# A recurrent state kernel with soft experts: the triangular solver on GpSimd, the first-half Gram by batch, a-tiles by ScalarE and a new order

## The chip, the cores and the metric

The kernel runs on one core of a Trainium2 chip. Its engines are TensorE (PE in the profile; PEld is its weight load), VectorE (DVE), ScalarE (ACT), GpSimd (POOL) and SyncE (SP), which issues nearly all loads. The metric is the device time of one execution in microseconds (us).

## The reference, cut to what matters

```python
# r, k, v, w, a, b: (4, 8, 768, 40), fp32;  B, H, S, D = 4, 8, 768, 40
for t in range(S):
    y[:, :, t] = einsum('bhd,bhde->bhe', r_t, state)
    Sa = einsum('bhde,bhe->bhd', state, a_t)
    state = state * w_t[:, :, None, :] - einsum('bhd,bhe->bhde', Sa, b_t) \
            + einsum('bhd,bhe->bhde', v_t, k_t)
x = y.transpose(0, 2, 1, 3).reshape(3072, 320)
logits = x @ phi                                   # 8 experts x 4 slots
d = softmax(logits over the rows); slot_input = d.T @ x
slot_out[e] = relu(slot_input[e] @ w1[e]) @ w2[e]  # 320 -> 1024 -> 320
out = softmax(logits over the slots) @ slot_out
```

## The kernel before, in words

The 768 steps are cut into 12 stages of 64 (NST; index st), and each stage into two halves of 32 (index q). The 32 pairs of batch and head are worked on in three groups u of 3, 3 and 2 heads (NHU) with all four batches, so that a group's 120 or 80 channels stand on the partitions. Two stages make a super-stage ss of 128 steps, for which one solve is made.

Per stage the pieces are these.

- prep_items (scan_s, scan_k, scan_c): the running products of the decays by two TENSOR_TENSOR_SCANs on DVE, and three multiplications of 120x768 that scale k, b and a, on POOL but for the first stages.
- bda_at, bdr_at: block-diagonal copies of the a- and r-tiles (one head's 40 channels in its own block). For a, bd_mult makes them by three ACT multiplications with a mask in stages under BM, and bd_load by DMAs from SBUF in the others. For r it is always bd_load.
- lgram and gram: products of k and b with a. lgram gives the triangular systems (32x32, one for each batch, head and half). gram gives the rest: rows 0 to 95 for the second half of the stage, rows 96 to 127 for the first. A mask multiplication on DVE takes them from PSUM to the tile qls.
- solve_in, solve_step, solve_out: the inverse of the triangular systems of a super-stage. solve_in transposes them on DVE (STREAM_TRANSPOSE), ACT copies, 30 steps follow that each have a multiplication and an addition of i x (31 - i) elements, and solve_out transposes back. The columns 0 to JP-1 of a step are done by POOL, the others by DVE. JP is 3 for solve 0, 7 for solve 1 and 2 for solves 2 to 5.
- chain_g, chain_u (for both halves) and chain_s: the recurrence from stage to stage. chain_g reads the old state, qls and the v-tile vus, chain_u multiplies with the solved inverse, and ACT copies its result into vus; chain_s makes the new state. chain_s adds the old state to PSUM into an SBUF temporary (wt_next) and multiplies that with the decays pms.
- y_vut, y_sd, y_p, y_y: the outputs of the stage before. slots_*: every second stage, the soft-expert statistics. After the last stage come the expert matmuls and the output.

Operations aren't issued as they are written. A class Plan records them, each with its engine, an estimated duration and what it depends on. Its schedule then simulates the engines: at each step it takes the engine that can start first, and of that engine's ready operations the one of highest prio (the length of the longest path behind it). What it finds is emitted in that order, so that each engine's queue is in order of the simulated start. The written order (run_all with the windows WIN, WIN0 and PRO) decides only which operation comes first where two share a buffer. Where the plan sees PE idle, fill puts in filler matmuls on constants (lines L462 and L466). fetch models PE's instruction loading, and pace holds loads back. Nearly all other instructions bear the line of the emitting helper, L1174 in the profile.

Of the kernel before, what the change touches and what calls it, by code (L numbers as in the profile page):

```python
# [23 lines left out]
NU = 3  # L24
# [5 lines left out]
JP = (3, 7, 2)  # L30

WIN = dict(cg=(0, 0.304, 0.4, 0.601, 0.759, 1), vl=(0.623, 0.633), ct=(0, 0.01), pr=(0.17, 0.795), ba=(0.926, 0.933),
           lw=(0.991, 1), lg=(0.121, 0.307), gr=(0, 0.404), kt=(0.696, 1), yv=(0.003, 0.4), ys=(0, 0.565), yp=(0.233,
# [3 lines left out]
            ba=(0.824, 1.778), lw=(0.869, 1.012), br=(0.133, 0.821), s0=(0.643, 1.33))  # L37
KV = 3
BM, AV = 6, 2
# [59 lines left out]


class Op:
    __slots__ = ("eng", "calls", "acc", "banks", "mode", "occ", "lat", "pred", "succ", "prio", "n", "ready", "alt", "at",
                 "done", "kind", "dma", "tag", "lanes", "boost", "turn", "rec", "after")
# [41 lines left out]
class Plan:  # L145
    def __init__(self, nc, tc, banks):
        self.nc, self.tc, self.banks = nc, tc, banks
        self.ops, self.open = [], None
        self.tensor, self.vector, self.scalar, self.gpsimd, self.sync, self.either = (
            Engine(self, n) for n in ("PE", "DVE", "ACT", "POOL", "SP", "EITHER"))  # L150
        self.live, self.masks, self.tag, self.boost = {}, {}, "", 0
# [28 lines left out]
    def record(self, eng, method, a, k):  # L180
# [11 lines left out]
        if new:  # L192
            o = Op()
            o.eng, o.calls, o.acc, o.banks, o.mode, o.kind, o.dma, o.tag, o.alt = eng, [], {}, set(), mode, method, 0, self.tag, None
            o.rec, o.after = 0, None
# [23 lines left out]
        if eng == "PE":  # L219
            o.occ = self.pe_add(o, cost, lane) + 170  # L220
            o.rec += 2 if method == "transpose" or "r" in str(a[1].dtype).split(".")[-1].replace("float", "") else 4
        else:
            self.costs(o, eng, method, a, k)
# [3 lines left out]
    def pe_cost(self, method, a):  # L227
# [13 lines left out]
        return (cls(kk), c), two * max(nn * (0.862 if two == 2 else 0.45), 8 * 4 / len(lane) if c == 32 else 45), lane  # L241
# [7 lines left out]
    def costs(self, o, eng, method, a, k):  # L249
        out = a[0]  # L250
        n = 1
        for s in out.shape[1:]:
            n *= s
        src = a[1] if len(a) > 1 and not isinstance(a[1], (int, float)) else None
# [11 lines left out]
        if eng == "DVE":  # L266
            if method == "transpose":
                dve = 2130 * n / 1024
            elif method == "tensor_tensor_scan":
                dve = 155 + 2.08 * n  # L270
            elif method == "tensor_reduce":
                dve += 0
            o.occ = dve
        elif eng == "ACT":
            if method == "activation" and not isinstance(k.get("scale", 1.0), float):
                act = 270 + 0.835 * n
            o.occ = act
        elif eng == "POOL":
            o.occ = 180 + (0.75 if method == "memset" else 1.97) * n
            if n < 300 and method == "tensor_tensor":  # L280
                o.occ += 40
        else:
            o.alt = dict(ACT=act, DVE=dve)
            o.occ = act


    def depend(self):
# [18 lines left out]
        for o in reversed(self.ops):  # L306
            d = o.occ + (2000 + o.dma / 215 if o.dma else 0)
            o.prio = d + o.boost + max((s.prio + SEM.get(o.eng + s.eng, 0) for s in o.succ), default=0)

    def schedule(self):  # L310
        self.depend()
        engs = ("PE", "DVE", "ACT", "POOL", "SP")
# [10 lines left out]
        def add(o):  # L323
            e = "ACT" if o.alt else o.eng
            o.ready = max((p.done + SEM.get(p.eng + e, 0) for p in o.pred), default=0.0)
            for e in ("ACT", "DVE") if o.alt else (o.eng,):
                cand[e].add(o)

        for o in self.ops:
            for b in o.banks:  # L330
                b.left += 1
# [3 lines left out]
        while len(order) < len(self.ops):  # L335
# [6 lines left out]
            def when(o, e):  # L342

                if o.dma:
                    return max(o.ready, self.pace(o)[0])
                if e != "PE":
                    return o.ready
                for b in o.banks:
                    if b.place is None:
# [3 lines left out]
                        r = max(o.ready, bf)  # L353
# [11 lines left out]
                return o.ready  # L365
# [14 lines left out]
            t, e = best  # L380
            ok = []
            for o in cand[e]:
                r = when(o, e)
                if r is not None and r <= t + 1e-6:
# [12 lines left out]

            if o.alt:

                e = min(("ACT", "DVE"), key=lambda x: start(o, x) + o.alt[x])  # L400
                cand["ACT"].discard(o)
                cand["DVE"].discard(o)
# [5 lines left out]
            if e == "PE":  # L408
                t, o.occ = self.fetch(o, t, free[e], dma_free)
                for b in o.banks:  # L410
                    if b.place is None:
# [3 lines left out]
                        held[b.place].append([t, None, max(m.bit_length() for x in b.ops for r in x.acc.get((b, True), ()) for m in r[2:])])  # L415
# [27 lines left out]
        import os  # L443
        if os.environ.get("PLAN"):
            print("plan", self.span, busy, len(self.ops), "stall", self.stall, "PE instructions", self.seen)
        return self.order

    def fill(self, gaps, held):

        self.extra = {}  # L450
        there = max(o.done for o in self.ops if o.dma and (self.idle[1].tensor.name, True) in o.acc)
        for a, b, p, o in gaps:

            i = next((i for i, h in enumerate(held) if all(y <= a or x >= b or c <= 384 for x, y, c in h)), None)
            n = int((b - a) * FILL[1] / (225 if a > WARM else 400))
            if i is not None and n:
                self.extra[o] = (n, p.mode if p else (128, 128), self.banks[i][:, 384:512], self.idle[a > there])

# [9 lines left out]
    def fetch(self, o, t, free, dma):  # L468

        gap = t - free  # L470
        n = int(gap * FILL[1] / 225) if gap > FILL[0] else 0
        for k, a, b in ((2 * n, free, t), (o.rec, t, t + o.occ - 165)):
# [3 lines left out]
            while left > 0:  # L476
# [5 lines left out]
                if (self.seen - FETCH[1]) % FETCH[0] == 0:  # L482
                    i = (self.seen - FETCH[1]) // FETCH[0]
                    prev = self.there[-1] if self.there else 0.0
                    self.there.append(max(x + FETCH[3] + min(FETCH[5], max(0.0, dma - x)), prev + 500) + FETCH[4])
# [35 lines left out]
    def emit(self):  # L521
# [3 lines left out]
        with self.tc.manual_schedule():  # L525
            for o in self.order:
# [3 lines left out]
                for method, a, k, line in o.calls:  # L530
# [5 lines left out]
                    if o.alt:  # L536
# [34 lines left out]
def rwkv_softmoe(ctx, tc, kb, b2, aa, ww, rr, vv, consts, phi, w1, w2, out):  # L571
# [8 lines left out]
    cs_t = cst.tile([128, 419], F32, name="cs_t")  # L580
    mask_q = cs_t[:, 0:32]
    mask_l = cs_t[:, 32:64]
# [65 lines left out]
    with ExitStack() as ac:  # L648
# [22 lines left out]
        tmp_r = [part(2, n) for n in (200, 200, 240, 240)]  # L671
# [32 lines left out]
        sms, cms = (Ring(space(4) for _ in range(2)) for _ in range(2))  # L704
        n_wt = [0]
# [60 lines left out]
        def bd_load(key, bd, src):  # L766
# [47 lines left out]
        def gram(st, u):  # L814
            if u == 0:
                qls.put(st)
            nh = NHU[u]
# [38 lines left out]
        def solve_in(ss):  # L856
            lt, n_t = lt_a, n_a
            nc.vector.transpose(lt.rearrange("p i t -> p t i"), lls[ss].rearrange("p c h t -> p t (c h)"))
            jp = JP[min(ss, 2)]
            for eng, j0, j1 in ((nc.gpsimd, 0, jp), (nc.vector, jp, 32)):  # L860
# [4 lines left out]
        def solve_step(ss, i):  # L865
            lt, n_t = lt_a, n_a
            m = 31 - i
            jp = JP[min(ss, 2)]
            for eng, j0, j1, x in ((nc.gpsimd, 0, min(i, jp), 0), (nc.vector, jp, i, 2)):
# [25 lines left out]
        def chain_g(st, u, q):  # L895
# [8 lines left out]
            k = slice(96, 128) if q == 0 else slice(0, 96)  # L904
            for j in range(nh):
                for b in range(B):
                    h = 12 * u + b * nh + j
                    nc.tensor.matmul(gp[32 * b:32 * b + 32, j * D:(j + 1) * D], qls[st][k, h, :],
                                     vu[k, h * D:(h + 1) * D], start=(sold is None), stop=(sold is None or j == nh - 1))
# [18 lines left out]
        def chain_s(st, u):  # L928
# [284 lines left out]
        if True:  # L1213
# [8 lines left out]
                    (three(gram, 3), *w["g3"]), (three(kbtok, 3), *w["k3"]))  # L1222
# [4 lines left out]
        for st in range(NST):  # L1227
# [6 lines left out]
            if st == 0:  # L1234
                o += [(one(lambda: load_w(4), lambda: load_k(4)), *w["lo"]), (prep_items(4), *w["pr"]),
# [149 lines left out]
def layouts(inputs):  # L1385
# [4 lines left out]
    def chan(n, pad):  # L1390
# [3 lines left out]
        for u in range(NU):  # L1394
# [12 lines left out]
                         for u in range(NU)], axis=3)  # L1407

    vv = vv[:, [0, 1, 0]].reshape(NST, 96, -1)
    st = np.triu(np.ones((32, 32), f4), 1)  # L1410
    one = np.ones((32, 32), f4)
    mq = np.concatenate([one, one, st, st])
# [5 lines left out]
    consts = np.concatenate([mq, -np.concatenate([st] * 4), ms, np.eye(128, dtype=f4), bm, np.tile(eye, (4, 1)), np.tile(eye, (4, 4))],  # L1418
# [3 lines left out]
               rr=chan("r", 0), vv=vv, consts=consts, phi=phi, w1=inputs["moe_w1"], w2=inputs["moe_w2"])  # L1422
# [17 lines left out]
```

## Time and profile before

| | us |
|---|---|
| median of 3 runs | 475.67 |
| lowest, highest | 465.01, 476.42 |
| the profiled execution | 468.54 |
| its span, first to last instruction | 466.5 |
| PE busy | 395.2 (85%) |
| DVE busy | 327.7 (70%) |
| ACT busy | 208.8 (45%) |
| POOL busy | 205.2 (44%) |

Busy times are sums over the span and hide its stages: up to 100 us runs the prologue (loads, solves 0 and the start of 1, the first preps), from 100 to 320 us the stages with preps and solves, then the last stages, the experts and the output. Matmuls are pipelined, so a busy PE isn't one at its peak. A row of groups has line, engine, operation, output and inputs, shapes and count, then busy us and mean ns, then the idle time before and what ended it. A row of the timeline has start and length in us, and in brackets the idle time before it.

### The profile page before, as it was taken

The page shows a single profiled execution, that of the slowest core. Times are in us where ns is not written, and L with a number is a line of the kernel's source. Part 1 is how long each engine was busy: PE and PEld are TensorE (multiplying, and loading weights), DVE is VectorE, ACT ScalarE, POOL GpSimd, SP SyncE. Part 2 cuts the span into 40 slices and gives each one's busy share as a digit, 9 for nine tenths or more (in the row PEclk, how much of TensorE's full clock was granted, in tenths as well). Part 3 has the DMA queues.
Part 4 walks back from the last instruction along what each step waited for, and adds up shares of the span by engine and source line. Part 5 has one row for each costly group of instructions (what it writes and reads, how often), then busy time and mean ns, then how long its engine had stood idle before and what let it go on. Part 6 is the DMA issues. An engine that isn't in the chain of part 4 may idle for free.

```text
span 466.5 us, 21450 instructions
## 1 busy us (share of the span) xinstructions
PE 395.2 (85%) x9399; PEld 344.9 (74%) x9399; DVE 327.7 (70%) x746; ACT 208.8 (45%) x619; POOL 205.2 (44%) x410
## 2 busy tenths in 40 slices
PE   6788787888987998989999889998968989999910
PEld 6777676777886987979888878887967767745810
DVE  7789889899899899888799958971724235332210
ACT  1521524781644737157643737564426654312210
POOL 4576976988288248761389625840000000110000
PEclk9789889998999999879999999999989999989965
DMA  8996114011442523424334244576565754870176
GB/s 201 261 224 188 36 32 128 16 55 40 127 117 81 139 79 117 111 89 130 109 112 139 90 134 133 170 231 180 140 177 142 227 163 127 240 227 1 34 156 149
DMA packets 38762, 61.27 MB, mean 131 GB/s; under 512 B 4173, under 2 KB 26557, under 8 KB 38669
## 3 DMA queue, kind: packets, MB, share of 16 engines
q1 hardware_dynamic: 38669, 59.91, 46.5%
q8 instruction: 73, 1.20, 1.1%
q14 instruction: 20, 0.16, 0.1%
HBM read 54.00 MB, written 3.93 MB: 124 GB/s over the span
## 4 chain that ended last, share of the span: by engine, by line
PE 48%; DVE 25%; DMA 9%; ACT 5%; issue 5%; POOL 2%; SPq 1%; DVEq 0%; ACTq 0%; POOLq 0%
PE ps L1174 45%; DVE wt L1174 23%; ACT wt L1174 4%; PE ps L462 3%; DMA wt<-in_vv_dram 2%; POOL wt L1174 2%; DMA wt<-in_rr_dram 2%; DMA wt<-in_w_dram 2%; DMA wt<-in_kb_dram 2%; DVE mem L1174 2%; DMA wt<-in_ww_dram 1%; ACT mem L1174 1%; PE ps L466 1%; SPq L1174 1%; DMA wt<-wt 1%
## 5 line engine op out<-in xcount | busy, mean ns | idle before, releaser
L1174 PE MATMUL ps<-wt,wt 128*32 128x40 f32 (+9 forms) x4968 | 164.0, 224 | 16.2 <-issue 5.7
L1174 PEld LDWEIGHTS ps<-wt,wt 128*32 128x32 f32 (+7 forms) x4968 | 146.4, 118 | 30.2 <-issue 12.6
L1174 POOL TENSOR_TENSOR wt<-wt 128x30 f32<-128x30 f32 (+21 forms) x360 | 140.0, 389 | 59.1 <-ACT wt L1174 33.1
L1174 DVE TENSOR_TENSOR wt<-wt 128x180 f32<-128x180 f32 (+29 forms) x324 | 123.4, 381 | 7.7 <-ACT wt L1174 2.3
L1174 DVE TENSOR_TENSOR wt<-ps,cs_t 128x384 f32<-128x384 f32 (+2 forms) x120 | 62.1, 522 | 36.8 <-PE ps L1174 28.8
L1174 ACT ACTIVATE wt<-ps 32x120 f32<-32x120 f32 (+1 forms) x288 | 72.0, 250 | 24.8 <-PE ps L1174 17.3
L1174 POOL TENSOR_TENSOR wt<-wt,wt 120x768 f32<-120x768 f32 x32 | 55.7, 1749 | 48.9 <-DMA wt<-in_kb_dram 32.4
L1174 PE MATMUL ps<-cs_t,wt 120*128 120x120 f32 (+5 forms) x496 | 69.2, 274 | 7.8 <-DMA cs_t<-in_consts_dram 2.6
L1174 ACT COPY mem<-ps 120x512 f32<-120x512 f32 (+6 forms) x99 | 45.3, 480 | 67.1 <-PE ps L1174 64.5
L1174 ACT COPY wt<-ps 128x120 f32<-128x120 f32 (+3 forms) x116 | 37.9, 357 | 80.6 <-PE ps L1174 77.7
L1174 PE MATMUL ps<-wt,mem 128*32 128x160 f32 (+4 forms) x592 | 66.9, 313 | 8.3 <-DMA wt<-in_rr_dram 6.9
L1174 PEld LDWEIGHTS ps<-wt,mem 128*32 128x32 f32 (+4 forms) x592 | 55.4, 156 | 11.0 <-DVE wt L1174 3.9
L1174 PEld LDWEIGHTS ps<-cs_t,wt 120*128 120x128 f32 (+5 forms) x496 | 53.2, 141 | 12.8 <-issue 3.5
L1174 DVE TENSOR_TENSOR_SCAN wt<-wt,wt 120x780 f32<-120x780 f32 x24 | 45.4, 1900 | 4.5 <-POOL wt L1174 2.7
L1174 POOL MEMSET mem<- 128x2048 f32 x1 | 1.8, 1804 | 96.0 <-DVE mid L1174 96.0
L462 PE MATMUL ps<-cs_t 128*128 128x128 f32 x170 | 26.3, 301 | 3.7 <-DVE wt L1174 2.0
L1174 PE MATMUL ps<-wt 32*32 32x40 f32 x1536 | 25.2, 202 | 5.0 <-issue 2.4
L462 PEld LDWEIGHTS ps<-cs_t 128*128 128x128 f32 x170 | 23.2, 210 | 5.2 <-DVE wt L1174 2.1
L1174 PEld LDWEIGHTS ps<-wt 32*32 32x32 f32 x1536 | 19.1, 107 | 10.8 <-issue 3.8
L1174 PE MATMUL ps<-mem 120*32 120x120 f32 (+1 forms) x528 | 25.5, 264 | 0.0
L1174 DVE STREAM_TRANSPOSE wt<-wt 128x1024 f32<-128x1024 f32 x12 | 25.3, 2127 | 0.3
L1174 ACT COPY wt<-wt 120x768 f32<-120x768 f32 (+6 forms) x24 | 16.9, 729 | 18.7 <-DVE wt L1174 16.6
(89 smaller groups left out, 303.5 us busy)
## 6 DMA issues: line engine op xcount, KB each, us to landing
wt<-in_w_dram SPq DMA_DIRECT2D x16, 640.0 KB
wt<-in_kb_dram SPq DMA_DIRECT2D x36, 240.0 KB
wt<-in_w_dram SPq DMA_DIRECT2D x16, 512.0 KB
wt<-in_ww_dram SPq DMA_DIRECT2D x12, 366.6 KB
mem<-in_rr_dram SPq DMA_DIRECT2D x36, 120.0 KB
wt<-in_vv_dram SPq DMA_DIRECT2D x12, 320.0 KB
wt<-in_aa_dram SPq DMA_DIRECT2D x30, 120.0 KB
wt<-in_rr_dram SPq DMA_DIRECT2D x24, 120.0 KB
```

What stands on the lines that cost most here:

```text
L462: self.nc.tensor.matmul(bank, src, src, start=True, stop=True)
L466: self.nc.tensor.matmul(bank[i:i + 32], src[r, 0:32], src[r], start=True, stop=True)
L1174: nc.vector.memset(one_f, 0.0)
```

## The change

1. Solver: JP becomes (3, 7, 32, 32, 32, 32). Solves 2 to 5 are done by POOL alone, with scratch tiles of 240 elements.
2. gram: the first-half product of batch b goes to rows 32b to 32b+31 and to columns behind the others, with a tile q0s and a mask multiplication of its own; chain_g of the first half reads q0s and a second copy of v by batch (vq, one buffer). Of v, a stage loads 64 rows in two DMAs, without the 32 rows that were repeated, and vq in a third.
3. BM = NST: the a-tiles of all stages are made by ACT.
4. bd_load (now for r alone) loads each group's heads by themselves: eight DMAs instead of three.
5. chain_s adds in place in PSUM and multiplies from there. The temporaries hold q0s and vq now.
6. gram of stage 3 is written in stage 0 instead of the prologue; the windows br of stage 0 and gr are others.
7. The plan: other constants (FETCH, FILL, ISSUE); CLASH holds a DVE operation without PSUM operands until POOL's last such one is done but for 138 ns, and the other way round (190 ns); an engine may take a more urgent operation that is ready up to 130 ns later (LOOK); PE may take a short one in front of an instruction-loading stall (NARROW); fillers only in gaps over 900 ns, less by 500 ns; and 32 random changes, by their seeds, are added to the priorities.

```diff
-JP = (3, 7, 2)
+JP = (3, 7, 32, 32, 32, 32)
...
-BM, AV = 6, 2
+BM, AV = NST, 2
...
-FETCH = (256, 96, 440, 1500, 2900, 3500)
-WARM = 9000
-FILL = (300, 0.8)
-
-ISSUE = 350
+FETCH = (256, 96, 410, 1300, 2400, 4500)
+FILL = (900, 500, 225)
+
+CLASH = dict(DVE=138, POOL=190)
+
+ISSUE = 420
...
+ROUNDS = 0
+SEEDS = (3, 21, 44, 62, 119, 136, 146, 166, 184, 236, 383, 839, 894, 1144, 1277, 1468, 1487, 1602, 1732, 2303, 3675, 4128,
+         4356, 4549, 5379, 5493, 5729, 5909, 5921, 5968, 6052, 6159)
...
+LOOK = dict(PE=1, DVE=130, ACT=1, POOL=130, SP=1)
+NARROW = (150, 24, 8000)
...
     def schedule(self):
         self.depend()
+        for o, x in zip(self.ops, sum((self.noise(n) for n in SEEDS), 0 * self.noise(0))):
+            o.prio += x
...
+    def noise(self, seed):
+        r, n = np.random.default_rng(seed), len(self.ops)
+        mode, s = r.integers(4), 10 ** r.uniform(2.7, 4.3)
+        if mode == 0:
+            return r.normal(0, s, n)
...
                 if e != "PE":
-                    return o.ready
+                    p = last.get("POOL" if e == "DVE" else "DVE") if o.clash else None
+                    return max(o.ready[e], p.done - CLASH[e]) if p and p.clash else o.ready[e]
...
+    def fillers(self, gap):
+        return int((gap - FILL[1]) / FILL[2]) if gap > FILL[0] else 0
...
-            for j in range(3):
-                g = B * sum(n > j for n in NHU)
-                load(bd[40 * j:40 * j + 40, j, 0:g], src[40 * j:40 * j + 40, 0:g], nc.sync)
+            for u in range(NU):
+                g = slice(B * u, B * u + B)
+                for j in range(NHU[u]):
+                    load(bd[40 * j:40 * j + 40, j, g], src[40 * j:40 * j + 40, g])
...
             for b in range(B):
-                nc.tensor.matmul(gr[96:128, b * w:(b + 1) * w], kbt(st)[0:n, B * u + b, 0, 0], bd[0:n, 0:nh, b, 0:32], start=True, stop=True)
+                nc.tensor.matmul(gr[32 * b:32 * b + 32, 4 * w:5 * w], kbt(st)[0:n, B * u + b, 0, 0], bd[0:n, 0:nh, b, 0:32], start=True, stop=True)
             nc.vector.tensor_tensor(
-                qls[st][:, 12 * u:12 * u + 4 * nh], gr[:, 0:4 * w].rearrange("p (h t) -> p h t", t=32),
-                mask_q.unsqueeze(1).broadcast_to([128, 4 * nh, 32]), ALU.mult)
+                qls[st][0:96, 12 * u:12 * u + 4 * nh], gr[0:96, 0:4 * w].rearrange("p (h t) -> p h t", t=32),
+                mask_q[0:96].unsqueeze(1).broadcast_to([96, 4 * nh, 32]), ALU.mult)
+            nc.vector.tensor_tensor(
+                q0s[st][:, H0[u]:H0[u] + nh], gr[:, 4 * w:5 * w].rearrange("p (h t) -> p h t", t=32),
+                mask_s.unsqueeze(1).broadcast_to([128, nh, 32]), ALU.mult)
...
-            load(vu[0:32], vv[st, 0:32])
-            load(vu[64:128], vv[st, 32:96])
+            for q in range(2):
+                load(vu[64 * q:64 * q + 32], vv[st, 32 * q:32 * q + 32])
+            load(vqs.put(st), vq[st])
...
-                wt = wt_next()
-                nc.vector.tensor_tensor(wt[0:n, 0:4 * n], sp[0:n, 0:4 * n], sold[0:n, cols(u)], ALU.add)
-                nc.vector.tensor_tensor(v4(snew[0:n, cols(u)]), v4(wt[0:n, 0:4 * n]), pmb, ALU.mult)
+                nc.vector.tensor_tensor(sp[0:n, 0:4 * n], sp[0:n, 0:4 * n], sold[0:n, cols(u)], ALU.add)
+                nc.vector.tensor_tensor(v4(snew[0:n, cols(u)]), v4(sp[0:n, 0:4 * n]), pmb, ALU.mult)
```

More of the change, by code (lines that the diff above doesn't have):

```diff
@@ L145, with __init__ @@
 class Plan:
-    def __init__(self, nc, tc, banks):
-        self.nc, self.tc, self.banks = nc, tc, banks
+    def __init__(self, nc, tc, banks, own=()):
+        self.nc, self.tc, self.banks, self.own = nc, tc, banks, {t.tensor.name for t in own}
         self.ops, self.open = [], None
-        self.tensor, self.vector, self.scalar, self.gpsimd, self.sync, self.either = (
-            Engine(self, n) for n in ("PE", "DVE", "ACT", "POOL", "SP", "EITHER"))
+        self.tensor, self.vector, self.scalar, self.gpsimd, self.sync, self.either, self.both = (
+            Engine(self, n) for n in ("PE", "DVE", "ACT", "POOL", "SP", "DVE ACT", "DVE POOL"))
         self.live, self.masks, self.tag, self.boost = {}, {}, "", 0
@@ L253, in costs @@
             n *= s
+        o.clash = ("DVE" in eng or eng == "POOL") and "ACT" not in eng and method != "transpose" and (
+            not o.banks) and not any(
+            x.tensor.name in self.own for x in aps if hasattr(x, "tensor"))
         src = a[1] if len(a) > 1 and not isinstance(a[1], (int, float)) else None
@@ L265, in costs @@
         act = 160 + 0.835 * n
[L266 to L284, printed above, removed]
+        if method == "transpose":
+            dve = 2130 * n / 1024
+        elif method == "tensor_tensor_scan":
+            dve = 155 + 2.08 * n
+        if method == "activation" and not isinstance(k.get("scale", 1.0), float):
+            act = 270 + 0.835 * n
+        pool = 180 + (0.75 if method == "memset" else 1.97) * n
+        cost = dict(ACT=act, DVE=dve, POOL=pool)
+        e = eng.split()
+        o.occ = cost[e[-1]]
+        if len(e) > 1:
+            o.alt = {x: cost[x] for x in e}
+            o.eng, o.occ = e[0], cost[e[0]]
     def depend(self):
@@ L311, in schedule, with backward, forward @@
         self.depend()
+        best, spans = None, []
+        for o, x in zip(self.ops, sum((self.noise(n) for n in SEEDS), 0 * self.noise(0))):
+            o.prio += x
+        for i in range(ROUNDS + 1):
+            self.forward()
+            spans.append(round(self.span))
+            if best is None or self.span < best[0]:
+                best = (self.span, [(o, o.at, o.done, o.occ, o.eng, o.after) for o in self.order],
+                        [(b, b.place) for b in self.tenants], self.extra, self.order)
+            if i < ROUNDS:
+                self.backward()
+        self.span, ops, places, self.extra, self.order = best
+        for o, *x in ops:
+            o.at, o.done, o.occ, o.eng, o.after = x
+        for b, b.place in places:
+            pass
+        self.spans = spans
+    def noise(self, seed):
+        import numpy as np
+        names = sorted({o.who for o in self.ops})
+        who = np.array([names.index(o.who) for o in self.ops])
+        r, n = np.random.default_rng(seed), len(self.ops)
+        mode, s = r.integers(4), 10 ** r.uniform(2.7, 4.3)
+        if mode == 0:
+            return r.normal(0, s, n)
+        v, w = np.zeros(n), r.integers(len(names))
+        if mode == 1:
+            v[who == w] = r.normal(0, s)
+        elif mode == 2:
+            i = np.where(who == w)[0]
+            a = r.integers(len(i))
+            v[i[a:a + 1 + r.integers(len(i) // 6 + 1)]] = r.normal(0, s)
+        else:
+            v = r.normal(0, s, n) * (r.random(n) < 0.05)
+        return v
+    def backward(self):
+        nxt, late = {}, {}
+        for o in sorted(self.ops, key=lambda o: (-o.done, -o.at)):
+            t = min((late[s] - SEM.get(o.eng + s.eng, 0) for s in o.succ), default=self.span)
+            if o.eng != "SP":
+                t = min(t, nxt.get(o.eng, self.span))
+            late[o] = t - (o.done - o.at)
+            nxt[o.eng] = late[o] - (LINE[o.eng] if o.eng != "SP" else 0)
+            o.prio = -late[o]
+    def forward(self):
         engs = ("PE", "DVE", "ACT", "POOL", "SP")
@@ L323, in add @@
         def add(o):
-            e = "ACT" if o.alt else o.eng
-            o.ready = max((p.done + SEM.get(p.eng + e, 0) for p in o.pred), default=0.0)
-            for e in ("ACT", "DVE") if o.alt else (o.eng,):
+            o.ready = {}
+            for e in o.alt or (o.eng,):
+                o.ready[e] = max((p.done + SEM.get(p.eng + e, 0) for p in o.pred), default=0.0)
                 cand[e].add(o)
+        self.tenants = []
         for o in self.ops:
             for b in o.banks:
-                b.left += 1
+                b.place, b.left = None, len(b.ops)
+            if o.cost:
+                o.occ, o.after = o.cost, None
+        for o in self.ops:
             if not left[o]:
@@ L390, in schedule @@
                     o = max(same, key=lambda x: (x.prio, -x.n))
-            def start(o, e):
-                p = last.get(e)
-                if p is None or e == "SP":
-                    return max(free[e], when(o, e))
-                turn = o.mode != p.mode if e == "PE" else (o.turn or p.turn)
-                return max(p.done + (TURN if turn else LINE)[e], when(o, e))
+            if e == "PE" and self.wait(o, start(o, e), free[e], dma_free) > NARROW[0]:
+                few = [x for x in ok if x.rec <= NARROW[1] and x.prio > o.prio - NARROW[2]
+                       and not self.wait(x, start(x, e), free[e], dma_free)]
+                if few:
+                    o = max(few, key=lambda x: (x.prio, -x.n))
             if o.alt:
-                e = min(("ACT", "DVE"), key=lambda x: start(o, x) + o.alt[x])
-                cand["ACT"].discard(o)
-                cand["DVE"].discard(o)
+                e = min(o.alt, key=lambda x: start(o, x) + o.alt[x])
+                for x in o.alt:
+                    cand[x].discard(o)
                 o.eng = e
@@ L414, in schedule @@
                         b.place = f[1]
-                        held[b.place].append([t, None, max(m.bit_length() for x in b.ops for r in x.acc.get((b, True), ()) for m in r[2:])])
+                        self.tenants.append(b)
+                        held[b.place].append([t, None, b.width()])
                 if t - free[e] > FILL[0]:
@@ L442, in schedule @@
         self.span, self.busy = max(o.done for o in order), busy
[L443 to L446, printed above, removed]
     def fill(self, gaps, held):
@@ L451, in fill, with wait @@
         there = max(o.done for o in self.ops if o.dma and (self.idle[1].tensor.name, True) in o.acc)
+        first = max(o.at for o in self.ops if o.kind == "memset" and o.calls[0][1][0] is self.idle[0])
         for a, b, p, o in gaps:
+            if o.at < first:
+                continue
             i = next((i for i, h in enumerate(held) if all(y <= a or x >= b or c <= 384 for x, y, c in h)), None)
-            n = int((b - a) * FILL[1] / (225 if a > WARM else 400))
+            n = self.fillers(b - a)
             if i is not None and n:
                 self.extra[o] = (n, p.mode if p else (128, 128), self.banks[i][:, 384:512], self.idle[a > there])
+    def fillers(self, gap):
+        return int((gap - FILL[1]) / FILL[2]) if gap > FILL[0] else 0
+    def wait(self, o, t, free, dma):
+        was = self.seen, list(self.there), self.stall, o.occ
+        self.fetch(o, t, free, dma)
+        lost = self.stall - was[2]
+        self.seen, self.there, self.stall, o.occ = was
+        return lost
     def filler(self, n, mode, bank, src):
@@ L468, in fetch @@
     def fetch(self, o, t, free, dma):
-        gap = t - free
-        n = int(gap * FILL[1] / 225) if gap > FILL[0] else 0
+        n = self.fillers(t - free)
         for k, a, b in ((2 * n, free, t), (o.rec, t, t + o.occ - 165)):
@@ L535, in emit @@
                     k = {n: self.place(x) for n, x in k.items()}
-                    if o.alt:
+                    if o.alt and "ACT" in o.alt:
                         s = k.get("scale")
@@ L704, in rwkv_softmoe @@
         sms, cms = (Ring(space(4) for _ in range(2)) for _ in range(2))
+        q0s = Ring(ht(t) for t in (part(3, 256), wts_t.tiles[0][:, 0:256], wts_t.tiles[0][:, 256:512]))
+        vqs = Ring([wts_t.tiles[1][:, 0:320]])
         n_wt = [0]
@@ L816, in gram @@
                 qls.put(st)
+                q0s.put(st)
             nh = NHU[u]
```

77 lines of the change are left out of this document (48 added, 29 removed).

## The prediction

> **What bounds the kernel now.** I read the page's busy shares and slices first, then the windows, the transposes that open and close each solve, and the chain. (In all rows L1174 is the helper that emits; operations are told apart by tiles and shapes.)
>
> ```profile
> span 466.5 us, 21450 instructions
> ...
> PE 395.2 (85%) x9399; PEld 344.9 (74%) x9399; DVE 327.7 (70%) x746; ACT 208.8 (45%) x619; POOL 205.2 (44%) x410
> ...
> DVE  7789889899899899888799958971724235332210
> POOL 4576976988288248761389625840000000110000
> ```
>
> The shares are averages over different stages. DVE is nearly full up to slice 27 and light behind it; POOL stops there too. So I cut the span at 100 us (end of the prologue) and 320 us (nearly the end of the last solve), and ask for the filler matmuls (L462, L466) alone in the same stretches:
>
> ```profile
> 0.00:100.00 100.00, 79.21 (x1572) 73.95 (x1572) 87.63 (x146) 42.51 (x99) 70.27 (x108) 0.91 0.51 130
> 100.00:320.00 220.00, 202.90 (x5246) 179.90 (x5248) 192.75 (x469) 117.36 (x373) 131.64 (x298) 0.97 0.42 120
> 320.00:466.50 146.50, 113.14 (x2595) 91.06 (x2583) 47.34 (x133) 48.90 (x149) 3.26 (x5) 0.91 0.54 149
> ...
> 100.00:320.00 220.00, 4.86 (x32) 4.09 (x32) 0.97 0.42 120
> ...
> 100.00:320.00 220.00, 2.09 (x72) 1.95 (x76) 0.97 0.42 120
> ```
>
> Columns: stretch, length, then PE, PEld, DVE, ACT, POOL busy; the last two rows are the fillers of the middle. There PE does 202.9 - 4.9 - 2.1 = 196 us of real work in 220 (89%) and DVE 192.8 (88%); both are near their limit. In the last 146 us PE alone matters.
>
> The solves give the beat of the middle. A pair of stages needs one solve, which ends in a STREAM_TRANSPOSE:
>
> ```profile
> 117.85 4.14 DVE L1174 STREAM_TRANSPOSE wt<-wt 128x1024 f32<-128x1024 f32 x2
> ...
> 164.57 2.18 DVE L1174 STREAM_TRANSPOSE wt<-wt 128x1024 f32<-128x1024 f32 x1
> ...
> 268.06 2.13 DVE L1174 STREAM_TRANSPOSE wt<-wt 128x1024 f32<-128x1024 f32 x1
> ...
> 330.51 2.15 DVE L1174 STREAM_TRANSPOSE wt<-wt 128x1024 f32<-128x1024 f32 x1
> ```
>
> Outputs of solve 1, 2, 4 and 5. Four pairs take 330.5 - 117.8 = 212.7 us, 53.2 each on average, but unevenly: 46.7 for the first, 62.5 for the last. The chain that ended last is shared in the same way:
>
> ```profile
> PE 48%; DVE 25%; DMA 9%; ACT 5%; issue 5%; POOL 2%; SPq 1%; DVEq 0%; ACTq 0%; POOLq 0%
> PE ps L1174 45%; DVE wt L1174 23%; ACT wt L1174 4%; PE ps L462 3%; DMA wt<-in_vv_dram 2%; POOL wt L1174 2%; DMA wt<-in_rr_dram 2%; DMA wt<-in_w_dram 2%; DMA wt<-in_kb_dram 2%; DVE mem L1174 2%; DMA wt<-in_ww_dram 1%; ACT mem L1174 1%; PE ps L466 1%; SPq L1174 1%; DMA wt<-wt 1%
> ```
>
> **The solver moves from DVE to GpSimd.** Solves 2 to 5 gave columns from 2 on to DVE; now POOL does all columns (JP 32). What DVE loses, what POOL pays:
>
> ```profile
> L1174 DVE TENSOR_TENSOR wt<-wt 128x28 f32<-128x28 f32 x16 | 4.2, 262 | 2.6 <-ACT wt L1174 2.3
> ...
> L1174 DVE TENSOR_TENSOR wt<-wt 128x210 f32<-128x210 f32 x16 | 8.1, 509 | 0.0
> ...
> L1174 POOL TENSOR_TENSOR wt<-wt 128x7 f32<-128x7 f32 x2 | 0.4, 209 | 0.2
> ...
> L1174 POOL TENSOR_TENSOR wt<-wt 128x161 f32<-128x161 f32 x2 | 1.0, 480 | 0.2
> ...
> L1174 POOL TENSOR_TENSOR wt<-wt 128x14 f32<-128x14 f32 x10 | 4.6, 463 | 0.7
> ...
> L1174 POOL TENSOR_TENSOR wt<-wt,wt 120x768 f32<-120x768 f32 x32 | 55.7, 1749 | 48.9 <-DMA wt<-in_kb_dram 32.4 <-DVE wt L1174 8.9 <-DMA wt<-in_b_dram 6.2
> ...
> 283.94 26.49 POOL L1174 TENSOR_TENSOR wt<-wt 128x30 f32<-128x30 f32 x59
> ```
>
> DVE: 14 shapes, 28 to 210 elements, x16 each (the first and last row are shown), 224 instructions that add up to 80.7 us, 20.2 a solve. POOL: from 7 to 161 elements the mean rises by 271 ns, 1.76 ns an element above some 197 ns. A solve has 60 instructions and 2 x sum of i(31-i) = 9920 elements: 60 x 0.197 + 9920 x 0.00176 = 29.3 us, and 0.08 us of idle before each (0.7 us for ten, fifth row) makes 34. The six prep multiplications of a pair (scaling k, b and a by the decays) add 6 x 1.75 = 10.5. So POOL needs 44.6 us of a pair undisturbed. It won't be: the last row has 59 small solver instructions in 26.5 us, 0.45 each, where size and gap explain 0.33. What disturbs them is seen here:
>
> ```profile
> 161.97 0.20 DVE L1174 TENSOR_TENSOR wt<-wt 128x28 f32<-128x28 f32 x1
> ...
> 162.43 3.38 POOL L1174 TENSOR_TENSOR wt<-wt,wt 120x768 f32<-120x768 f32 x2 [7.63 <-DMA wt<-in_kb_dram]
> ...
> 163.06 1.15 DVE L1174 TENSOR_TENSOR wt<-wt 128x28 f32<-128x28 f32 x1
> 164.10 0.55 DVE L1174 TENSOR_TENSOR wt<-ps,cs_t 128x384 f32<-128x384 f32 x1
> ...
> L1174 DVE TENSOR_TENSOR_SCAN wt<-wt,wt 120x780 f32<-120x780 f32 x24 | 45.4, 1900 | 4.5 <-POOL wt L1174 2.7 <-DMA wt<-in_ww_dram 1.8
> ```
>
> The same DVE instruction takes 0.20 us alone and 1.15 while POOL multiplies; one that reads PSUM takes its usual 0.55 beside the same POOL work. So DVE instructions with two SBUF inputs and POOL's exclude each other. By the Trainium skill, SBUF — State Buffer, section "Who interferes with whom", that is an exclusive lock for the whole instruction, taken by DVE only with two SBUF inputs or in a two-port mode; the trace agrees (1.15 against 0.20 and 0.55).
>
> After the change DVE has few such instructions left: four scans a pair, 7.6 us. POOL's pair thus lies between 44.6 and 44.6 + 7.6 = 52.2. PE needs 196 / 220 x 53.2 = 47.4, less what the Gram gives below. DVE falls from 46.6 (192.75 / 220 x 53.2) by 20 to some 28 and bounds nothing. The pair is then set by POOL, just ahead of PE: three pairs with prep at 51, the last without prep (34 + scans none) by PE and the chain at some 48: 201 against 212.7. **Term: -12 us**; bounds -28 (PE's 46 for all) and -4 (POOL's 52.2 for all).
>
> **First-half Gram by batch quadrants.** Four matmuls used to write the same 32 PSUM rows; now each batch has its own, as in lgram already:
>
> ```profile
> 20.02 0.87 PE L1174 MATMUL ps<-wt,wt 120*32 120x96 f32 x32
> ...
> 21.83 1.49 PE L1174 MATMUL ps<-wt,wt 120*32 120x96 f32 x16
> ...
> L1174 DVE TENSOR_TENSOR wt<-ps,cs_t 128x384 f32<-128x384 f32 x72 | 39.1, 548 | 24.5 <-PE ps L1174 17.1 <-ACT wt L1174 7.0
> ...
> L1174 DVE TENSOR_TENSOR wt<-ps,cs_t 128x256 f32<-128x256 f32 x36 | 14.9, 419 | 1.9 <-PE ps L1174 1.4
> ```
>
> The first row is lgram spread over four quadrants (27 ns each), the second gram on one (93 ns). So 16 instructions fall from 1.49 to some 0.44, with the smaller third group 1.4 us a stage: 2.8 of a pair (PE 44.6, counted in the bound above), nothing where PE waits anyway. The price is a second mask multiply: the two DVE rows rise by 1 ns an element, so 96 elements cost about 0.26 us, 1.4 us a pair, on an engine that was just relieved. The small matmuls of chain_g that read the new layout keep count and shape. Net beyond the pair: **0**, between -3 and +3.
>
> **The a-tiles by ACT; chain_s in PSUM; loads.** From stage 6 on three ACT multiplications replace three SBUF-to-SBUF loads:
>
> ```profile
> L1174 ACT ACTIVATE wt<-wt,bm_t 120x768 f32<-120x768 f32 (+1 forms) x18 | 14.4, 855 | 6.2 <-POOL wt L1174 5.1 <-PE ps L1174 1.2
> ...
> 180.15 2.36 DMA wt<-wt
> ```
>
> 6 x 3 x 0.855 = 15.4 us on ACT, which is 53% busy in the middle; behind them queue the copies of gp and up that the chain waits for, so up to 2.6 us a stage, 0 to +15. What goes is 18 loads, one of which stood on the chain with 2.4 us (and others like it may). I take **-1**. chain_s adds in place in PSUM, so two instructions become free of the lock and a bank is held one instruction longer: nothing (both ends +-2). SP issues five more loads a stage for r and one more for v, at 0.3 us a time; SP is no bound, but a later landing would show as PE waiting for r; the smaller pieces can also land earlier for the first group. The one buffer of vq makes its next load wait for the first-half chain_g of a stage, which comes early in it. **-1**, from -5 to +5.
>
> **Fillers and order.** Gaps must now pass 0.9 us, and their first 0.5 us stays empty. Fillers stand for 4% of the chain above, 18 us (3% L462, 1% L466); where they overran their gap the work behind them was late. I take a sixth, **-3**; bounds -18 and +6, the latter if the granted clock, 0.91 in the first 100 us against 0.97 in the middle, fell by that step over another 100 us. Gram 3 leaves the prologue for stage 0, with 2 x 0.55 + 0.42 = 1.5 us of masks on DVE, which the end of the prologue waits for at most: **-1**, from -1.5 to 0. The new order (the plan now knows the exclusion, looks 0.13 us ahead on DVE and POOL, and has 32 kept random changes) has no row of its own. PE is idle or filling for 51 us of the first 100 and some 50 of the last 146, so there is room; an in-order engine that is sent to wait at the wrong time loses as easily. I take 0, from -18 to +12.
>
> **Sum.** 468.5 (the profiled execution's own time, 2 us above its span) - 12 - 1 - 1 - 3 - 1 = 450.5. The median of the runs shown, 475.67, lies 1.5% above the profiled one, the lowest, 465.01, just under it; that scatter has no row, so I put the forecast a little up: **453 us**.
>
> **Rivals.**
> 1. *POOL becomes too slow (the slower side).* To 44.6 + 7.6 comes the hand-over: out-transpose, in-transpose, ACT's copy, and only then POOL:
>
> ```profile
> 171.85 1.53 POOL L1174 TENSOR_TENSOR wt<-wt 128x30 f32<-128x30 f32 x1 [6.04 <-ACT wt L1174]
> ```
>
> 6 us in which POOL idles unless a prep multiplication lies ready. Then a pair with prep takes 58 to 59, three of them 177 and the last 34 + 6 + 8 = 48: 225, 12 more than now, 481 us. It decides as soon as a pair passes 53.2; the first pair, 46.7 now, would suffer at once. For it: POOL runs no faster than its rows. Against: kb's prep can fill the hand-over, and DVE has lost the 224 instructions that held POOL up. The Trainium skill, GPSIMD Engine Reference, section "Engine selection", speaks for it: elementwise work with two inputs belongs on VectorE, GpSimd being about twice as slow; the rows here agree in part (1.76 ns an element against 1.0). Chance 0.13.
> 2. *PE was the bound all along.* Then only the Gram's 1.4 us for eight stages and some fillers come back, 11 + 3 us at most and mostly less: 460 to 470, within 2%. For it: 89% real PE work in the middle. Against: the last pair, 62.5 us, with PE and DVE no fuller than before. Chance 0.20.
> 3. *The order does nothing of what the plan promised*, since the plan's waits aren't the chip's; the DVE gain then goes into stalls elsewhere: 465 to 475. Chance 0.05.
> 4. *The order is worth more*: 10 to 18 us out of the idle first 100 and last 146: 432 to 443. Chance 0.20.
> My forecast (444 to 459) has 0.42.
>
> A measurement of this kernel can tell about 2% from no change. Faster by more: the forecast, rival 4 and a little of rival 2, 0.66; within 2%: 0.20; slower: rival 1 and a rest, 0.14. The range, 434 to 475, leaves out rival 1 and the end of rival 4.
>
> **What would show it.** Out-transposes of solves 1 to 5 some 50 us apart and evenly; DVE busy near 260 us and POOL near 265; no DVE solver shapes behind solve 1; 120*32 matmuls of gram at 27 ns; PE over 92% in the middle; no wt<-wt loads. Wrong if POOL is over 95% busy between the transposes with a beat above 53, or if PE waits for ACT copies (rows "PE ps <- ACT wt" above 10 us) or for in_rr.

## The result, and the profile after

| | before | changed |
|---|---|---|
| median of 4 runs, us | 472.85 | 447.06 |
| lowest, highest | 465.01, 476.42 | 444.82, 453.10 |
| span of the profiled execution | 466.5 | 443.0 |

The ratio is 0.955 (95% interval 0.948 to 0.962): faster by 4.5%. The forecast was 453 us, a ratio of 0.952 to 0.967 by the run it is held against; the time is right and, as the runs below show, its largest term stands at the wrong place. Executions that ran over 1.5% longer than the shortest, at a lower granted clock, count in the medians and not in the ratios.

The changed kernel's page, the lines that answer to those of before:

```profile
span 443.0 us, 21393 instructions
...
PE 376.9 (85%) x9411; PEld 317.3 (72%) x9411; DVE 267.3 (60%) x554; ACT 221.3 (50%) x633; POOL 242.8 (55%) x410
...
DVE  6869999789965377854479555646354542522400
POOL 3838884897288964788976889278810000200000
...
PE 66%; DVE 8%; ACT 7%; DMA 6%; issue 4%; POOL 3%; SPq 1%; ACTq 0%; POOLq 0%; DVEq 0%
```

DVE lost 60 us and is no longer full in the middle; POOL gained 38. On the chain that ended last, DVE fell from 25% to 8% and PE rose from 48% to 66%: PE is what the kernel now waits for.

The transposes that close solves 1 to 5 of the changed kernel (in each double row the in-transpose of the next solve follows at once):

```profile
117.14 4.05 DVE L1273 STREAM_TRANSPOSE wt<-wt 128x1024 f32<-128x1024 f32 x2
...
178.06 4.15 DVE L1273 STREAM_TRANSPOSE wt<-wt 128x1024 f32<-128x1024 f32 x2
...
230.37 4.19 DVE L1273 STREAM_TRANSPOSE wt<-wt 128x1024 f32<-128x1024 f32 x2
...
283.38 4.14 DVE L1273 STREAM_TRANSPOSE wt<-wt 128x1024 f32<-128x1024 f32 x2
...
326.60 2.10 DVE L1273 STREAM_TRANSPOSE wt<-wt 128x1024 f32<-128x1024 f32 x1
```

From 117.1 to 326.6 are 209.5 us; before it was 212.7. So the beat of the solves, where I had put 12 us, gave 3. Nor is it even: the four pairs take 60.9, 52.3, 53.0 and 43.2 us, where before the first was the shortest (46.7) and the last the longest (62.5). What the beat does hold is more work. Busy times from the first out-transpose to the last one, and behind it, of before and then of the changed kernel (columns: PE, PEld, DVE, ACT, POOL busy with counts):

```profile
117.85:330.50 212.65, 197.24 (x5332) 175.27 (x5334) 178.35 (x435) 114.81 (x364) 118.06 (x261) 0.98 0.44 127
330.50:466.50 136.00, 103.60 (x2283) 82.09 (x2271) 44.68 (x128) 45.39 (x137) 3.26 (x5) 0.90 0.54 149
```

```profile
117.14:326.60 209.46, 197.87 (x5546) 169.94 (x5547) 128.80 (x246) 125.74 (x378) 157.65 (x262) 0.99 0.44 124
326.60:443.00 116.40, 85.80 (x1678) 63.15 (x1676) 37.26 (x110) 40.41 (x121) 3.16 (x5) 0.88 0.56 154
```

The middle runs 214 matmuls more in 3 us less, with PE as busy as before; nearly all of them are real work, since the fillers there stay at 224 and 228. So 605 fewer are left behind the last solve, 86 of them fillers, and that part is 19.6 us shorter: 11 us of real PE work, 7 of fillers (12.5 before, 5.8 now) and 2 of idle time. More than half of the time was thus earned in the middle and shows at the end; the rest is gaps at the end that became smaller.

One Gram half of a stage (24 instructions, three groups) in the changed kernel:

```profile
225.78 0.66 PE L1273 MATMUL ps<-wt,wt 120*32 120x96 f32 x24
```

27 ns each as forecast, where the first two groups alone took 1.49 us. Without the fillers, the union of PE's busy time over the whole span fell from 348.7 to 335.2 us, by 13.5.

### The profile page after: what moved, and what is told of

It reads as the page before. It is cut to its first block, busy times and chain, and to the rows that moved or that the text cites. A ratio compares the mean times of both kernels' runs of the same rounds, so it can differ in the third digit from the quotient of the medians.

```text
span 443.0 us, 21393 instructions
## 1 busy us (share of the span) xinstructions
PE 376.9 (85%) x9411; PEld 317.3 (72%) x9411; DVE 267.3 (60%) x554; ACT 221.3 (50%) x633; POOL 242.8 (55%) x410
## 4 chain that ended last, share of the span: by engine, by line
PE 66%; DVE 8%; ACT 7%; DMA 6%; issue 4%; POOL 3%; SPq 1%; ACTq 0%; POOLq 0%; DVEq 0%
PE ps L1273 60%; DVE wt L1273 7%; ACT wt L1273 6%; POOL wt L1273 3%; PE ps L550 3%; PE ps L554 3%; DMA wt<-in_kb_dram 3%; DMA wt<-in_ww_dram 1%; DMA wt<-in_w_dram 1%; DVE mem L1273 1%; DMA wt<-in_aa_dram 1%; SPq L1273 1%; ACT mem L1273 1%; DMA wt<-in_rr_dram 0%; ACT mid L1273 0%
## 5 line engine op out<-in xcount | busy, mean ns | idle before, releaser
L1273 POOL TENSOR_TENSOR wt<-wt 128x30 f32<-128x30 f32 (+23 forms) x360 | 177.5, 493 | 58.7 <-ACT wt L1273 32.8
L1273 PE MATMUL ps<-wt,wt 128*32 128x40 f32 (+8 forms) x4200 | 134.3, 224 | 10.1 <-ACT wt L1273 4.0
L1273 PEld LDWEIGHTS ps<-wt,wt 128*32 128x32 f32 (+6 forms) x4200 | 114.4, 118 | 25.1 <-issue 8.1
L1273 DVE TENSOR_TENSOR wt<-ps,cs_t 128x384 f32<-128x384 f32 (+5 forms) x132 | 64.1, 498 | 49.3 <-PE ps L1273 39.0
L1273 PEld LDWEIGHTS ps<-cs_t,wt 120*128 120x128 f32 (+5 forms) x496 | 52.2, 140 | 21.9 <-issue 14.8
L1273 ACT COPY mem<-ps 120x480 f32<-120x480 f32 (+6 forms) x99 | 45.0, 480 | 40.9 <-PE ps L1273 32.1
L1273 DVE TENSOR_TENSOR wt<-wt 128x27 f32<-128x27 f32 (+25 forms) x100 | 41.4, 414 | 2.1
L1273 PE MATMUL ps<-mem 32*32 32x40 f32 (+2 forms) x1040 | 33.9, 232 | 3.4 <-issue 1.9
L1273 DVE TENSOR_TENSOR ps<-ps,wt 120x480 f32<-120x480 f32 (+1 forms) x30 | 18.1, 606 | 29.8 <-PE ps L1273 27.7
L1273 ACT ACTIVATE wt<-wt,bm_t 120x768 f32<-120x768 f32 (+1 forms) x36 | 28.5, 858 | 10.6 <-PE ps L1273 4.1
L1273 ACT COPY wt<-wt 120x768 f32<-120x768 f32 (+5 forms) x20 | 16.5, 836 | 21.4 <-DVE wt L1273 18.8
```

What stands on the lines that cost most here:

```text
L1273: nc.vector.memset(one_f, 0.0)
```

## The experiments

Each ratio is to the kernel before, run on the same chip beside it; 1% is about 4.7 us. A kernel that is planned anew gets another order of everything. So some runs keep the order of the changed kernel, instruction by instruction, and alter one thing in what is issued. Only these tell of a part by itself, and they tell it for that one order, which was tuned with all parts in place; what a part is worth in an order of its own they don't show. No run of either kind undoes chain_s in PSUM, the smaller loads or the new place of gram 3 alone.

### Parts undone, planned anew without the random changes

no_random:

```diff
-SEEDS = (3, 21, 44, 62, ...)
+SEEDS = ()
```

> The changed kernel without the 32 random changes to the priorities; all else stays. Theory ORDER (a large part of the gain is the tuned order): 8 to 15 us slower than the changed kernel's 447, so 455 to 462. Theory WORK (the gain is less PE work and a relieved DVE, whatever the order): 447 to 451.

0.979 (0.971 to 0.987), 461.8 us: the 32 kept changes are worth 2.4 points, 11 us, as theory ORDER had it (the two intervals don't touch).

gram_old, on top of it:

```diff
-                nc.tensor.matmul(gr[32 * b:32 * b + 32, 4 * w:5 * w], kbt(st)...
+                nc.tensor.matmul(gr[96:128, b * w:(b + 1) * w], kbt(st)...
```

> As no_random, but the first-half Gram is back on one quadrant (four matmuls one after another, one mask). Theory PE (TensorE bounds all stages behind the prologue): slower than no_random by what its real PE work grows, 13 to 16 us (1.4 us a stage). Theory DVE (the solver's move paid, the Gram is hidden): 0 to 4 us.

0.972 (0.965 to 0.979): no slower than no_random, which speaks for theory DVE, unless the new order itself made up for the work. PE does have more to do: without fillers its union is 349.7 us against 337.2 in no_random. The 12.5 us took the place of idle time and fillers. gram_serial below asks the same with the order held.

solver_dve, on top of no_random:

```diff
-JP = (3, 7, 32, 32, 32, 32)
+JP = (3, 7, 2, 2, 2, 2)
```

> As no_random, but solves 2 to 5 are back on VectorE but for two columns. Theory DVE: 10 to 20 us slower than no_random. Theory PE: within 5 us of no_random, since PE's work is the same; the time between the solves' out-transposes stays near 52 us a pair.

1.033 (1.025 to 1.041): 25 us slower than no_random, more than theory DVE asked for.

old_work (all parts undone, new plan):

```diff
+# JP, BM, gram, chain_s, bd_load, vload and the place of gram 3 as before; SEEDS = ()
```

> The work of the kernel before (solver, Gram, a-tiles, chain_s, loads, place of gram 3) under the plan of the changed kernel without the random changes. Theory ORDER: the plan's new rules alone bring 8 us or more, 455 to 462 where the kernel before has 468 to 473. Theory WORK: 466 to 474, as the kernel before.

1.073 (1.066 to 1.079), 504 us. Both expectations miss it. The first order that the new plan finds for the old work is 7% worse than the old plan's, so the new rules alone bring it nothing. What they bring to the new work, no run tells.

bd_dma, on top of no_random:

```diff
-BM, AV = NST, 2
+BM, AV = 6, 2
```

> As no_random, but the a-tiles from stage 6 on come by DMA again. By the prediction's step the ACT version is worth 1 us, so 459 to 466 here; if a load's landing time held the Gram up, 8 us or more slower than no_random, 470 and over.

1.037 (1.028 to 1.046): 19 us slower than no_random by the medians, 27 by the ratios. The two ran on different chips, and beside bd_dma, before_solver and other_random the ratios go by 464 us for the kernel before, where its median is 470. So these three ratios may be a point or more too high. PE's waits for the loads, which no_random doesn't have, are 6.9 us of it:

```profile
PE ps L1272 <- DMA wt<-wt: 6.9, 9, 1.1
```

The rest is not separated from the other order.

before_solver, in the kernel before:

```diff
-JP = (3, 7, 2)
+JP = (3, 7, 32)
...
-        tmp_r = [part(2, n) for n in (200, 200, 240, 240)]
+        tmp_r = [part(2, n) for n in (240, 240, 240, 240)]
```

> The kernel before with its own plan, changed in one thing: solves 2 to 5 wholly on GpSimd. If the solver's move pays by itself, as VectorE's relief does in the changed kernel: 8 to 20 us faster than before. If it pays only together with a plan that knows the exclusion between the two engines: within 5 us of before, or slower.

1.028 (1.007 to 1.048), 1.017 by the medians: somewhat slower, though by how much is unclear, and not 8 to 20 us faster. The solver's move alone, under the old plan, gains nothing. Whether that is the missing rule of exclusion or just an order that fits badly, this run doesn't say.

other_random, blind numbers instead of the kept ones:

```diff
-SEEDS = (3, 21, 44, 62, ...)
+SEEDS = tuple(range(7001, 7033))
```

> The changed kernel with 32 other random changes, taken blindly (the next numbers in a row) instead of the kept ones. If the gain of the kept ones is their selection, a blind set lies no better than none: 457 to 480. If random priorities help as such, 447 to 455. Its distance from no_random (462) is also a measure of how far two orders of the same work lie apart.

1.033 (1.014 to 1.052), 479 us: a blind set is no better than none, as expected if the gain lies in the selection. So the same work in three orders takes 447, 462 and 479 us. This is also the measure for the comparisons above: a part that is undone and planned anew moves the time by its own worth and by some 17 us of order (no_random against other_random, 25 by the ratios), either way. The 25 us of solver_dve are hardly more than that, and what bd_dma lost is no more.

### The same order, one thing altered

solver_dve_same_order:

```diff
-                eng = engines[o.eng]
+                eng = self.nc.vector if getattr(o, "lat", 0) > 1 else engines[o.eng]
```

Here lat is the number of the solve that an instruction belongs to.

> The changed kernel, every instruction in its place in the order, but the solver instructions of solves 2 to 5 are issued on VectorE. Theory DVE (the relief of VectorE pays): 15 to 40 us slower, 460 to 490. Theory POOL: the solver gets shorter on VectorE (some 20 us against 34), so within 8 us of the changed kernel or faster.

0.994 (0.987 to 1.000): 3.9 points slower than the changed kernel, 18 us. DVE's relief pays, in the middle alone:

```profile
116.30:344.80 228.50, 205.83 (x5550) 175.33 (x5550) 199.43 (x487) 126.87 (x380) 31.56 (x22) 0.96 0.38 113
344.80:462.50 117.70, 87.42 (x1675) 62.71 (x1673) 37.41 (x109) 40.32 (x121) 3.17 (x5) 0.87 0.55 154
```

Stretches as above. DVE is busy 199 of 228.5 us again, the middle is 19 us longer and what follows only 1. PE, with the same work, is idle 11 us longer there and busy 8 us longer, at a granted clock of 0.96 instead of 0.99; whether the clock fell because PE idled, the run doesn't show.

pool_short:

```diff
+                    if getattr(o, "lat", 0) > 1 and a[0].shape[1] > 2:
+                        a = [x[:, 0:2] if hasattr(x, "ap") else x for x in a]
                     i = at_line(line, f, a, k)
```

> The changed kernel, every instruction in its order, but GpSimd's solver instructions of solves 2 to 5 work on two columns at most, so the inverse is left incomplete: 2560 elements a solve instead of 9920, 13 us less POOL work of each pair. Theory POOL (GpSimd sets the beat of the middle, 52 us a pair): the out-transposes come 4 to 6 us a pair closer and the time falls by 12 to 25, to 422 to 435. Theory PE: the beat stays and the time falls by under 5.

0.949 (0.943 to 0.956), not to be told from the changed kernel. This is what decides: 12 to 25 us less were asked for. The profiled execution took 452 us, 2% more than the shortest (443), so its stretches are some 2% too long:

```profile
119.50:333.70 214.20, 200.85 (x5546) 172.31 (x5547) 129.64 (x247) 125.84 (x378) 95.88 (x262) 0.98 0.43 123
```

POOL does 62 us less, and the middle has none of the 16 to 24 us less that theory POOL asks for (214 us, some 210 without the 2%, against 209.5). Theory POOL falls. The trace of the changed kernel had it already, at the end of solve 4, in POOL's own timeline and in DVE's:

```profile
278.61 1.34 POOL L1273 TENSOR_TENSOR wt<-wt 128x58 f32<-128x58 f32 x4
288.88 11.48 POOL L1273 TENSOR_TENSOR wt<-wt 128x30 f32<-128x30 f32 x22 [8.92 <-ACT wt L1273]
```

```profile
282.58 0.69 DVE L1273 TENSOR_TENSOR wt<-ps,cs_t 128x512 f32<-128x512 f32 x1 [3.43 <-PE ps L1273]
283.38 4.14 DVE L1273 STREAM_TRANSPOSE wt<-wt 128x1024 f32<-128x1024 f32 x2
```

POOL is done at 280.0, but DVE transposes only at 283.4: it first had to take an operation that waited 3.4 us for PE. POOL idles 8.9 us, and part of that is PE's.

gram_serial:

```diff
+                    if o.eng == "PE" and method == "matmul" and "gram" in o.who and "lgram" not in o.who and a[0].shape[0] == 32:
+                        h = a[0]
+                        a[0] = bass.AP(tensor=h.tensor, offset=h.offset - h.offset // h.ap[0][0] * h.ap[0][0], ap=[[h.ap[0][0], 128]] + [list(d) for d in h.ap[1:]])
+                        l = a[1]
+                        a[1] = bass.AP(tensor=l.tensor, offset=l.offset, ap=[list(l.ap[0]), [1, 128]])
                     i = at_line(line, f, a, k)
```

> The changed kernel, every instruction in its order, but each of gram's four first-half matmuls writes all 128 rows, one over the other, so they run one after another as before the change (values of that tile are lost). PE gets some 16 us of work back. Theory PE: 10 to 16 us slower, 457 to 463. Theory DVE: 0 to 5 us.

1.001 (0.996 to 1.006): 4.6 points, 22 us slower. PE's sum on its page and the two stretches:

```profile
PE 402.1 (86%) x9411; PEld 342.9 (74%) x9411; DVE 268.2 (58%) x554; ACT 221.3 (47%) x633; POOL 238.1 (51%) x410
```

```profile
124.70:349.20 224.50, 213.79 (x5549) 186.12 (x5548) 131.74 (x246) 126.46 (x380) 157.05 (x262) 0.99 0.39 115
349.20:465.90 116.70, 85.96 (x1679) 62.31 (x1676) 37.28 (x110) 40.41 (x121) 3.17 (x5) 0.88 0.55 155
```

PE has 25.2 us more to do, more than the 16 I meant to give back (a full-row instruction of 96 columns takes some 130 ns there, 93 on one quadrant before), and 22 of them are in the time: 0.87 us for each us of PE. Of the longer span, 7.6 us lie in front of the first out-transpose (124.7 against 117.1), where PE has 9 us more to do, and 15 in the middle, where it has 16. The part behind the last solve has no Gram and hasn't moved. So with the order held PE bounds the middle, and the 13.5 us that the real change took from PE are worth some 12 in this order (an estimate: 13.5 x 0.87). In gram_old, in its other order, they aren't seen in the time.

no_fill:

```diff
-        self.fill(gaps, held)
+        self.extra = {}
```

> The changed kernel, every instruction in its order, without the filler matmuls. If they overrun their gaps, the time falls by 2 to 6 us; if the granted clock needs them, it falls below 0.93 and the time rises by 4 to 15 us.

0.953 (0.946 to 0.961): no change. The granted clock falls,

```profile
core 0: 440.3 us, clock 0.914
```

from 0.963, and nothing comes of it. The low digits lie in slices 4 to 8, and one in slice 12:

```profile
PEclk9996577899968999999998999999999989979965
...
33.00:89.00 56.00, 32.09 (x706) 27.54 (x707) 49.65 (x103) 24.02 (x70) 42.96 (x83) 0.70 0.27 75
...
117.36 3.82 DVE L1273 STREAM_TRANSPOSE wt<-wt 128x1024 f32<-128x1024 f32 x2
```

In slices 4 to 8 (the second row; columns as above, and behind POOL the clock, 0.70) PE is busy for 32 of 56 us and DVE for 50, so PE has room to run slower. Solve 1 closes at 117.4 us, as with the fillers (117.1).

### A better version

If the order is worth as much as the parts, another search should find more. I started from no random change and kept each number whose addition shortened the plan's own span, up to 35.

```diff
-SEEDS = (3, 21, 44, 62, ...)
+SEEDS = (3, 6, 19, 21, 73, 99, 546, 696, 902, ..., 7766, 7767, 7907, 8137)
```

> The changed kernel with another set of random changes: 35 that were kept one by one, from none on, because each shortened the plan's own span; nothing else differs. Theory ORDER (an order that the plan finds shorter is shorter on the chip, and TensorE's idle time is what it closes): 438 to 446, a ratio to the kernel before of 0.93 to 0.955. Theory LUCK (the kept set of the change happened to suit the chip): like no random changes or a blind set, 455 to 480.

0.926 (0.916 to 0.936): faster than the changed kernel (0.948 to 0.962), with the work unchanged. The seven executions took 429 to 442 us, median 438.8. The ratio goes by 429 to 433; by the medians of all it is 0.938 against 0.945 of the changed kernel, so how much faster is less sure than that it is. Theory LUCK falls; theory ORDER had its lower bound at 438. That it is TensorE's idle time which the shorter order closes, as that theory says, isn't shown.

## Why the prediction was right, point by point

**The solver, -12.** DVE's relief is real and larger: 18 us with the order held, an order tuned for the solver on POOL. The term's mechanism failed at the step "the pair is then set by POOL, just ahead of PE". POOL's prices were right (619 ns forecast for 240 elements, 643 measured below), but pool_short takes 62 us from POOL and nothing changes, while gram_serial gives PE 16 us in the middle and 15 come back in its time. PE sets the pair. I had both numbers, 44.6 to 52.2 for POOL and 44.6 for PE, and believed the upper one, although PE's real work at 89% of the middle stood under the first table. PE's 44.6 supposed that it is packed without a gap; in the changed kernel the middle has 24 us in which PE idles or runs fillers, 6 us a pair.

```profile
L1273 POOL TENSOR_TENSOR wt<-wt 128x240 f32<-128x240 f32 x16 | 10.3, 643 | 1.3
```

The form in which the gain came was wrong too: I looked for a shorter and even beat. The solves came 3 us sooner and held some 210 real matmuls more; the end was shorter by 20. Of the other signs, DVE's 267 us and the Gram's 27 ns came as named; POOL stayed at 243 us instead of 265, and PE's 94% of the middle is 88% without the fillers, as before.

**The Gram, 0.** This term was mis-sized. The price of 27 ns came out, the work that it saves too (13.5 us), but I let it count only as a lower bound of PE's pair. With PE as the bound it is worth about 12, in this order; planned anew without the random changes, gram_old, it is worth nothing that can be seen. Rival 2 was right about PE in the changed kernel. That PE was the bound all along isn't shown: no run undoes the Gram in the kernel before, and solver_dve_same_order shows DVE as a bound too, which rival 2 had left out.

**ACT, loads, -2.** PE's waits for the r-tiles, of before in its list of waits, and of the changed kernel in the view of the loads' tile:

```profile
PE ps L1174 <- DMA wt<-in_rr_dram: 6.9, 3, 3.5
```

```profile
  PE ps L1273: 0.3, 1
```

From 6.9 us to 0.3, so the r-tiles did land in time; whether by the smaller pieces or by the new order isn't separated. Undone with a new plan the ACT version seems worth 19 us, of which 6.9 is seen as waits for the loads, while the order alone can move as much. The term was probably too small; by how much is open.

**Fillers, -3.** The fillers that are left cost nothing, by no_fill: without them PE just waits. They are not much fewer, 45.5 us of PE time against 53.3, and on the chain they went from 4% to 6% without costing anything, so a share of the chain was no price. What the old rule's fillers cost in the old order, no run tells. The fear for the clock was empty: it is 1.00 in the first 100 us of the changed kernel, against 0.91 before.

**Order, 0 with -18 to +12.** The random changes give -11. The rest of the term, the plan's new rules, has no run with the new work. The range held it, but a term of this size is no remainder: it is as large as each of the parts.

**The sum.** -18 forecast, -23.5 in the two spans. Taken with the order held, solver 18 and Gram 12 are already more than the gain, and order 11 comes on top. So they don't add; that each uses the same idle time of PE, and that the parts were planned together with the order, are likely reasons that no run separates. That the total came out near is in part luck: a solver term that was too small and a Gram and an order put at nothing were made up for by their not adding.

**Rival 1** (POOL too slow) didn't happen. The hand-over of 6 to 9 us is there, as drawn, and the first pair did grow, from 46.7 to 60.9 us; but with POOL's work cut, in pool_short, it still takes 61.6 (119.5 to 181.0), so POOL isn't why. The Trainium skill's rule in GPSIMD Engine Reference, section "Engine selection", is borne out in the prices (1.7 to 1.8 ns an element on POOL against 1.0 on DVE: medians of 266 and 632 ns for 30 and 240 elements in the changed kernel, 189 and 397 on DVE in solver_dve_same_order) and not in the outcome: the slower engine was the one with time to spare. By the exclusion that the Trainium skill's page SBUF — State Buffer, section "Who interferes with whom", states, DVE's work on PSUM runs beside POOL's; the prediction's row of 0.55 us agrees. Such work is most of what DVE kept in the middle, some 87 us of 135 when its instructions are added up.

## What to carry to other kernels

Two engines near 90% in the same stretch are to be taken as one bound: here, with DVE relieved and the order held, nearly every microsecond of PE counted (0.87 us for each), so a part that looked hidden came close to its full price. Move work to the engine that has idle time even if it is slower at it, but before you call that engine the next bound, shorten its work in the same order and see whether the time follows. Where a planner orders the queues, undoing a part and planning anew measures the order as much as the part; hold the order and alter one instruction as well, and remember that this prices the part in that one order.

## What was not expected of the hardware

TensorE's granted clock fell from 0.963 to 0.914 on the mean without the filler matmuls, and the time stayed where it was (0.953 against 0.955). The same matmuls with 128 output rows instead of 32 on four quadrants cost far more than their number says: 24 Gram instructions of a stage became dearer by 25.2 us in 12 stages, 2.1 us a stage.
